# Sink-window attention and a gated feed-forward on one core: weight loads from GpSimd's queue, idle products at the start, and the first 256 tokens of all four sequences first

## Chip, cores and metric

One core of a Trainium2 chip. The metric is device time in microseconds of one execution of the program. Engines: PE (TensorE, products; PEld its weight loads), DVE (VectorE), ACT (ScalarE), POOL (GpSimd), SP (SyncE, which issues most transfers).

## The reference

Attention over 4 sequences x 8 heads x 768 tokens x 64 dimensions, float32. A token sees the first `n_sink` tokens and a window of the last `window` ones. Then a feed-forward over all 3072 tokens:

```
keep   = (col < n_sink) | ((0 <= row - col) & (row - col < window))
a      = softmax(where(keep, q @ k.T / 8, -1e9));  x = concat of heads of a @ v     # 3072 x 512
h      = x @ w_in                                # 512 x 2048
out    = (h * clip(h + 3, 0, 6) / 6) @ w_out     # 2048 x 512
```

`n_sink` (4) and `window` (128) are run-time values. The weights arrive as 64-bit floats.

## The kernel before

**Units and slots.** The tokens are cut into 12 units, a unit being 256 tokens of one sequence: (b, 0), (b, 1), (b, 2). A unit's 8 heads are taken as 4 pairs, and one pair of one unit is a *slot* of the attention, so there are 48 slots, `pus`. The list `units` sets their order: (0, 0) and (1, 0) lead, then sequence by sequence what is left. First units (u = 0) have 2 blocks of keys, scores of 128 and 256 columns for the two query tiles, and no sink part; later units have scores of 2 x 272 columns, a third block of keys, and the sinks by products of their own (`D_snk`, ssc, pz). Eight slots (s < 8, u = 0) are `plain`: they multiply in float32, which takes two passes a product. All others split each operand into two float32r parts, hi and lo (`split_parts`), by ACT and DVE, and copy K and Q within SBUF to both halves of the partitions (lines 247 and 260; K and Q have one buffer each).

**Order of the work.** A loop over s (line 534) runs the steps of one string; C is the scores and softmax of slot s - 1, E the products with V of slot s - 2, D the transposes of slot s - 1, L, V, Bk and Bq the loads and splits of slots s and s + 1, W the weight loads, and each "-" runs one step of the feed-forward:

```
ORDER = "V C00 - C01 E0 - C10 - C11 E1 L - Bk - Bq W - D0 - S D1 -"
MULT = [1] * 12
WN = [0, 1, 1, 1, 1, 4, 4, 4, 4, 4, 4, 4]
```

So there are 8 feed-forward steps a slot, taken from queues that a unit joins when its last pair has left E (line 528). A step is half of `ffn1` (12 products of 256 columns, hps, line 437) or half of `ffn2` (6 products of 512 columns, o, line 457); a unit has 34 steps. A step comes only when the weights that it needs have been placed in the program (line 496). What is left after slot 47 runs at the end, products alone.

**Weights.** 32 loads of 512 KB (`load_part`, lines 134 to 161): one in each of slots 1 to 4, four in each of slots 5 to 11. A load is issued by SP into one of three buffers st (shared with the output tile ost), and then turned from 64-bit into two float32r parts: two steps on ACT (lines 150 and 154), two on DVE (line 156, which moves the sign with a 16-bit AND, and line 158), the high part by ACT (line 35), the low part by DVE (line 161). SP's queue is in order; a load that waits for a free st stands ahead of the loads of kr, qr, vr (lines 217, 218, 232) and the copies of K and Q.

**Start.** GpSimd writes rel, col and the identity (lines 65 to 72); n_sink and window come by two transfers on ACT's queue (lines 79 and 80, tile raw); DVE makes the masks from them (lines 82 to 113), and GpSimd the masks m_t0 and m_t1 of the later units and two clearings (vs, ssc; lines 177 and 178). Seven small steps for the flag fl (lines 563 to 570), which chooses a general path at the end, run here too, as nothing holds them back.

Of the kernel before, what the change touches and what calls it, by code (L numbers as in the profile page):

```python
# [9 lines left out]
F32 = mybir.dt.float32  # L10
F32R = mybir.dt.float32r
I32 = mybir.dt.int32
BF16 = mybir.dt.bfloat16
U16 = mybir.dt.uint16
U32 = mybir.dt.uint32
ALU = mybir.AluOpType
AF = mybir.ActivationFunctionType
# [2 lines left out]
P = 128  # L20
SK = 16
WMAX = 128
SCALE = 0.125
BIG = 1.0e30


def split_parts(nc, hi, lo, src, hi_engine, lo_engine):

    copy_r(nc, hi_engine, hi, src)
    lo_engine.tensor_tensor(out=lo, in0=src, in1=hi.bitcast(F32), op=ALU.subtract)  # L30


def copy_r(nc, eng, out, src, scale=1.0):
    if eng is nc.scalar:
        nc.scalar.mul(out=out, in_=src, mul=scale)  # L35
    elif eng is nc.gpsimd:
        nc.gpsimd.tensor_scalar(out=out, in0=src, scalar1=scale, scalar2=1.0, op0=ALU.mult, op1=ALU.mult)
    elif scale != 1.0:
        nc.vector.tensor_scalar(out=out, in0=src, scalar1=scale, scalar2=None, op0=ALU.mult)
    else:  # L40
        nc.vector.tensor_copy(out=out, in_=src)  # L41
# [3 lines left out]
def attn_ffn_kernel(ctx: ExitStack, tc: tile.TileContext, qx, kx, vx, vfx, vsx, n_sink, window, w_in, w_out, out):  # L45
    nc = tc.nc
    B, NU, NP = qx.shape[0:3]
# [7 lines left out]
    const = ctx.enter_context(tc.tile_pool(name="const", bufs=1))  # L55
    fast = ExitStack()
    work = fast.enter_context(tc.tile_pool(name="work", bufs=2))
    ps = fast.enter_context(tc.tile_pool(name="ps", bufs=8, space=PSUM))
# [4 lines left out]
    relf = rel.rearrange("p a b -> p (a b)")  # L63
# [3 lines left out]
    nc.gpsimd.iota(colf[:, 0:P], pattern=[[1, P]], base=0, channel_multiplier=0,  # L67
                   allow_small_or_imprecise_dtypes=True)
    ident_r = const.tile([P, P], F32R, name="ident_r")
    ident0 = work.tile([P, P], F32, tag="st", name="ident0", bufs=3)  # L70
    make_identity(nc, ident0)
    nc.gpsimd.tensor_copy(out=ident_r, in_=ident0)
    ident = ident_r.bitcast(F32)
    three = const.tile([P, 1], F32, name="three")
    nc.vector.memset(three, 3.0)


    raw = const.tile([P, 2, 2], I32, name="raw")
    nc.scalar.dma_start(out=raw[:, 0, :], in_=n_sink.bitcast(I32).partition_broadcast(P))
    nc.scalar.dma_start(out=raw[:, 1, :], in_=window.bitcast(I32).partition_broadcast(P))  # L80
    rawf = const.tile([P, 2, 2], F32, name="rawf")
    nc.vector.tensor_copy(out=rawf, in_=raw)
    neg = const.tile([P, 2], F32, name="neg")
# [4 lines left out]
                                   op0=ALU.mult, op1=ALU.add)  # L88
# [3 lines left out]
    W2 = 2 * P + SK  # L92
    WP = 2 * P + 2 * SK
    m_t0 = work.tile([P, W2], BF16, name="m_t0", bufs=1)
    m_t1 = work.tile([P, W2], BF16, name="m_t1", bufs=1)
# [3 lines left out]
    own, prev, snk = relf[:, P:2 * P], relf[:, 2 * P:3 * P], colf[:, P:2 * P]  # L99
# [6 lines left out]
    def bias_from(dst, keep, engine=nc.vector):  # L106
        engine.tensor_scalar(out=dst, in0=keep, scalar1=-1.0, scalar2=BIG, op0=ALU.add, op1=ALU.mult)

# [2 lines left out]
    nc.vector.tensor_tensor(out=tmpm, in0=prev, in1=snk, op=ALU.max)  # L111
    bias_from(m_01[:, 0:P], tmpm)
    bias_from(m_01[:, P:2 * P], own)
    bias_from(m_t0[:, 0:P], prev, nc.gpsimd)
    bias_from(m_t0[:, P:2 * P], own, nc.gpsimd)
    bias_from(m_t0[:, 2 * P:W2], snk[:, 0:SK], nc.gpsimd)
    nc.gpsimd.tensor_copy(out=m_t1[:, 0:P], in_=m_t0[:, 0:P])
    nc.gpsimd.tensor_copy(out=m_t1[:, P:P + SK], in_=m_t0[:, 2 * P:W2])
    nc.gpsimd.tensor_copy(out=m_t1[:, P + SK:W2], in_=m_t0[:, P:2 * P])


    WIH = [const.tile([P, NP, 256], F32R, name=f"wih{i}") for i in range(NFP)]
# [6 lines left out]
    def weng(which, at):  # L129
        return {"D": nc.vector, "P": nc.gpsimd, "A": nc.scalar}[which[at % len(which)]]  # L130

    def load_part(hi, lo, src, rows, at):

        def like(t):
            return t.rearrange("p (a b) -> p a b", a=rows)

        if not wide:
            st = like(work.tile([P, 512], F32, tag="st", name="st", bufs=3))
            nc.sync.dma_start(out=st, in_=src)
            split_parts(nc, hi, lo, st, nc.scalar, nc.vector)  # L140
            return
        st = work.tile([P, 512, 2], I32, tag="st", name="st", bufs=3)
        nc.sync.dma_start(out=like(st.rearrange("p n w -> p (n w)")), in_=src.bitcast(I32))
        it = work.tile([P, 512], I32, tag="wt", name="wt", bufs=3)
        low, high = st[:, :, 0], st[:, :, 1]
        ft = it.bitcast(F32)
        half = st.rearrange("p n w -> p (n w)").bitcast(U16).rearrange("p (n w) -> p n w", w=4)


        nc.scalar.activation(out=ft, in_=high.bitcast(F32), func=AF.Abs, scale=2.0 ** -112)  # L150

        nc.scalar.activation(out=low, in_=low.bitcast(U32), func=AF.Copy, scale=2.0 ** -29 * (1 - 2.0 ** -18),
                             bias=7.5 * 2.0 ** -18 - 0.5)
        nc.vector.tensor_scalar(out=half[:, :, 1], in0=half[:, :, 3], scalar1=0x8000, scalar2=None,  # L156
                                op0=ALU.bitwise_and)
        nc.vector.scalar_tensor_tensor(out=it, in0=it, scalar=3, in1=low,  # L158
                                       op0=ALU.logical_shift_left, op1=ALU.bitwise_or)
        copy_r(nc, weng(WHI, at), hi, like(ft))  # L160
        weng(WLO, at).tensor_tensor(out=lo, in0=like(ft), in1=hi.bitcast(F32), op=ALU.subtract)  # L161
# [12 lines left out]

    vs = work.tile([P, NP, 4 * D], F32R, name="vs", bufs=1)
    ssc = work.tile([P, 2, P], F32R, name="ssc", bufs=1)
    nc.gpsimd.memset(vs.bitcast(F32), 0.0)
    nc.gpsimd.memset(ssc.bitcast(F32), 0.0)

    def batch_loads(b):  # L180
        v4 = vs[0:4 * SK].rearrange("p a (h d) -> p a h d", h=4)
# [10 lines left out]
    def eng(which, s):  # L192
        return {"D": nc.vector, "P": nc.gpsimd, "A": nc.scalar}[which[1 + (s % (len(which) - 1)) if s < START else 0]]

    first = [(0, 0), (1, 0)]
    units = first + [(b, u) for b in range(B) for u in range(NU) if (b, u) not in first]
    pus = [(b, u, p) for (b, u) in units for p in range(NP)]
    st_ = [dict() for _ in pus]
# [73 lines left out]
    def cell(s, h, t, c0, c1):  # L272

        if plain(s):
            return st_[s][f"P{h}"][:, t * P + c0:t * P + c1]
        return st_[s]["P"][:, h, t, c0:c1]
# [36 lines left out]
    def C_soft(s, h):  # L313
        b, u, p = pus[s]
        d = st_[s]
        nb, sm, rc = d["nb"], d["sm"], d["rc"]
        hs = slice(2 * h, 2 * h + 2)
        live = [(0, W2), (0, W2)] if u else [(0, P), (0, 2 * P)]
        for t in range(2):
            i, blk = 2 * h + t, cell(s, h, t, *live[t])  # L320
            nc.scalar.activation(out=blk, in_=blk, func=AF.Exp, scale=-1.0,  # L321
                                 bias=nb[:, i:i + 1], accum_out=sm[:, i:i + 1])
        nc.vector.tensor_scalar(out=sm[:, hs], in0=sm[:, hs], scalar1=1e-9, scalar2=None, op0=ALU.add)
        nc.vector.reciprocal(out=rc[:, hs], in_=sm[:, hs])  # L324
        for t in range(2):
            i, blk = 2 * h + t, cell(s, h, t, *live[t])
            norm((NORM0 if s < START else NORM)[i], blk, rc[:, i:i + 1])
        if u and h == 1:

            ss = ssc[:, :, 0:4 * SK].rearrange("p t (k h y) -> p t k h y", k=2, h=2)  # L330
            snk_in = d["P"].rearrange("p h t w -> p h (t w)")[:, :, 2 * P:2 * WP].rearrange(
                "p h (t y) -> p t h y", t=2)[:, :, :, 0:SK]
            split_parts(nc, ss[:, :, 0], ss[:, :, 1], snk_in, weng(SSE, 0), weng(SSE, 1))
# [181 lines left out]
    def slot_C(s, h, t):  # L515
        if 0 <= s < NS:
            C_score(s, h, t)
            if t == 1:
                C_soft(s, h)

    def slot_E(s, h):
        if 0 <= s < NS:
# [9 lines left out]
    WN = [0, 1, 1, 1, 1, 4, 4, 4, 4, 4, 4, 4]  # L532

    for s in range(NS + 2):
        for step in ORDER.split():
            if step == "-":
                drain(MULT[s] if s < len(MULT) else 1)
            elif step[0] == "C":
                slot_C(s - 1, int(step[1]), int(step[2]))
            elif step[0] == "E":  # L540
                slot_E(s - 2, int(step[1]))
            elif step == "V":
                if s < NS:
                    A_v(s)
                if 2 <= s and pus[s - 2][1:] == (1, 0):
                    batch_loads(pus[s - 2][0])
            elif step == "L" and s + 1 < NS and s > 0:
                A_kq(s + 1)
            elif step == "Bk" and 0 < s < NS:
                B_k(s)  # L550
            elif step == "Bq" and 0 < s < NS:
                B_q(s)
            elif step == "W":
                for _ in range(WN[s] if s < len(WN) else 0):
                    w_order.pop(0)()
            elif step[0] == "D" and 0 <= s - 1 < NS:
                D_pt(s - 1, int(step[1]))
            elif step == "S" and 0 <= s - 1 < NS:
                D_snk(s - 1)
    drain(sum(len(q) for q in queues))  # L560


    fl = const.tile([P, 4], F32, name="fl")
    nc.vector.tensor_scalar(out=fl[:, 0:1], in0=ns_f, scalar1=float(SK), scalar2=None, op0=ALU.is_gt)
    nc.vector.tensor_scalar(out=fl[:, 1:2], in0=win_f, scalar1=1.0, scalar2=None, op0=ALU.is_lt)
    nc.vector.tensor_scalar(out=fl[:, 2:3], in0=win_f, scalar1=float(WMAX), scalar2=None, op0=ALU.is_gt)
# [8 lines left out]
    with tc.If(flag == 1):  # L575
        with ExitStack() as gen:
# [71 lines left out]
            with tc.For_i(0, B, 1) as bi:  # L648
                for u in range(NU):
                    xn = gp.tile([P, NP, UT], F32, name="xn")  # L650
                    for c in range(NP):
                        nc.sync.dma_start(out=xn[:, c, :],
                                          in_=xv[ds(bi, 1), :, c, u * UT:(u + 1) * UT].rearrange("o p s -> (o p) s"))
# [75 lines left out]
```

## Time and profile before

| | us |
|---|---|
| median of 3 runs | 764.99 (764.61 to 767.12) |
| profiled execution | 765.18 |
| its span, first to last instruction | 763.3 |
| PE busy | 728.7 |
| DVE busy | 505.8 |
| ACT busy | 458.1 |
| POOL busy | 4.0 |

A busy PE need not be a PE at its peak: the ends of products are modelled and they overlap, so the number of products that start in a stretch tells more than the busy share. The granted clock is 1.00 at 2.4 GHz and 0.50 at 1.2 GHz. "Landing" is the end of a transfer after its issue.

### The profile page before, as it was taken

How to read it: one execution, taken by the hardware profiler on the slowest of the kernel's cores; microseconds unless marked ns; L12 is line 12 of the kernel's file. 1: busy time of each engine (PE TensorE's matmuls, PEld its weight loads, DVE VectorE, ACT ScalarE, POOL GpSimd, SP SyncE). 2: the span in 40 equal slices, each digit the busy share in tenths (PEclk: the TensorE clock that was granted, in tenths of full speed). 3: DMA queues.
4: the chain of work that ended last, by engine and by line, in shares of the span. 5: the costliest groups of instructions: out<-in, count | busy, mean ns of one | idle time of the engine just before them, and what ended most of it. 6: DMA issues, size and time to landing. Idle time of an engine off the chain costs nothing.

```text
span 763.3 us, 13907 instructions
## 1 busy us (share of the span) xinstructions
PE 728.7 (95%) x4832; PEld 648.1 (85%) x4832; DVE 505.8 (66%) x1434; ACT 458.1 (60%) x1115; POOL 4.0 (1%) x17
## 2 busy tenths in 40 slices
PE   4999888889999999999999999999999999999996
PEld 2677677679999999999889999899889989999895
DVE  4679999967677766765776776765676776542331
ACT  4788889776766755755666666755665665511211
POOL 2000000000000000000000000000000000000000
PEclk9999999999999999999999999999999999999998
DMA  5456878455454544532644545434554442000000
GB/s 187 121 165 217 238 212 237 138 142 132 128 134 122 134 125 105 140 95 67 166 110 114 143 107 127 120 82 102 146 130 116 128 114 72 15 15 1 28 1 32
DMA packets 57134, 89.87 MB, mean 118 GB/s; under 512 B 8672, under 2 KB 40416, under 8 KB 57056
## 3 DMA queue, kind: packets, MB, share of 16 engines
q1 hardware_dynamic: 56768, 88.90, 43.1%
q8 instruction: 40, 0.66, 0.4%
q14 instruction: 38, 0.31, 0.1%
q10 hardware_dynamic: 288, 0.00, 0.0%
HBM read 41.68 MB, written 6.29 MB: 63 GB/s over the span
## 4 chain that ended last, share of the span: by engine, by line
PE 78%; DVE 10%; ACT 5%; DMA 3%; issue 2%; SPq 1%; ACTq 0%; DVEq 0%
PE o L457 30%; PE hps L437 30%; PE av L399 7%; PE pt L341 4%; PE sp L297 4%; PE sp L292 2%; DMA K<-kt 1%; ACT Pt L307 1%; DVE st L156 1%; ACT Pt L321 1%; DVE wt L158 1%; DVE gf L444 1%; DVE Pt L299 1%; DMA raw<-in_window_dram 1%; DVE g L446 1%
## 5 line engine op out<-in xcount | busy, mean ns | idle before, releaser
L437 PE MATMUL hps<-xh,wih 128*128 128x256 f32 x768 | 219.9, 286 | 2.1 <-ACT wih L35 1.9
L437 PE MATMUL hps<-xh,wil 128*128 128x256 f32 x768 | 216.1, 282 | 1.6 <-DVE wil L161 1.6
L437 PE MATMUL hps<-xl,wih 128*128 128x256 f32 x768 | 215.5, 281 | 0.0
L457 PE MATMUL o<-woh,gh 128*128 128x512 f32 x384 | 156.2, 407 | 6.6 <-DVE gh L41 2.4
L457 PE MATMUL o<-woh,g 128*128 128x512 f32 x384 | 152.8, 399 | 1.9 <-DVE g L446 1.9
L457 PE MATMUL o<-wol,gh 128*128 128x512 f32 x384 | 152.5, 397 | 0.0
L437 PEld LDWEIGHTS hps<-xh,wih 128*128 128x128 f32 x768 | 145.7, 190 | 5.3 <-ACT wih L35 3.9
L437 PEld LDWEIGHTS hps<-xh,wil 128*128 128x128 f32 x768 | 145.2, 189 | 3.4 <-DVE wil L161 3.3
L437 PEld LDWEIGHTS hps<-xl,wih 128*128 128x128 f32 x768 | 145.6, 190 | 1.4
L321 ACT ACTIVATE Pt<-Pt,nb 128x272 f32<-128x272 f32 (+2 forms) x160 | 81.1, 507 | 73.3 <-DVE nb L299 71.3
L443 ACT ACTIVATE gf<-hps,three 128x512 f32<-128x512 f32 x96 | 65.9, 686 | 88.9 <-PE hps L437 88.4
L444 DVE SCALAR_TENSOR_TENSOR gf<-gf,hps 128x512 f32<-128x512 f32 x96 | 66.0, 687 | 67.0 <-ACT gf L443 65.8
L457 PEld LDWEIGHTS o<-woh,g 128*128 128x128 f32 x384 | 72.6, 189 | 21.8 <-DVE g L446 5.1
L457 PEld LDWEIGHTS o<-woh,gh 128*128 128x128 f32 x384 | 72.6, 189 | 19.1 <-DVE gh L41 3.1
L299 DVE CUSTOM_DVE_ANT_0 Pt<-sp,m_t 128x272 f32<-128x272 f32 x128 | 55.8, 439 | 49.5 <-PE sp L297 49.0
L307 ACT ACTIVATE Pt<-Pt,rc 128x272 f32<-128x272 f32 (+2 forms) x158 | 72.1, 502 | 25.9 <-DVE rc L324 24.7
L457 PEld LDWEIGHTS o<-wol,gh 128*128 128x128 f32 x384 | 72.6, 189 | 11.1 <-DVE wol L161 0.3
L446 DVE TENSOR_TENSOR g<-gf,gh 128x512 fp32r<-128x512 f32 x96 | 66.2, 690 | 1.1
L30 DVE TENSOR_TENSOR pl<-pt,ph 128x512 fp32r<-128x512 f32 (+1 forms) x80 | 52.8, 661 | 18.4 <-ACT ph L35 17.8
L297 PE MATMUL sp<-K,Q 128*128 128x272 f32 (+2 forms) x320 | 64.1, 288 | 0.7 <-DMA Q<-qt 0.4
L35 ACT ACTIVATE ph<-pt 128x512 fp32r<-128x512 f32 (+1 forms) x80 | 46.3, 578 | 29.5 <-PE pt L341 28.2
L297 PEld LDWEIGHTS sp<-K,Q 128*128 128x128 f32 x320 | 53.2, 189 | 8.1 <-DVE gf L444 0.7
(91 smaller groups left out, 944.0 us busy)
## 6 DMA issues: line engine op xcount, KB each, us to landing
K<-kt SPq DMA_DIRECT2D x128, 200.0 KB, 3.5
Q<-qt SPq DMA_DIRECT2D x160, 64.0 KB, 2.4
st<-in_w_in_dram SPq DMA_DIRECT2D x16, 512.0 KB, 4.7
st<-in_w_out_dram SPq DMA_DIRECT2D x16, 512.0 KB, 5.0
kr<-in_kx_dram SPq DMA_DIRECT2D x32, 200.0 KB, 2.6
qr<-in_qx_dram SPq DMA_DIRECT2D x48, 128.0 KB, 2.2
vr<-in_vx_dram SPq DMA_DIRECT2D x32, 192.0 KB, 2.6
out_dram<-ost SPq DMA_DIRECT2D x24, 256.0 KB, 2.3
```

The lines of the kernel that those rows point to most:

```text
L30: lo_engine.tensor_tensor(out=lo, in0=src, in1=hi.bitcast(F32), op=ALU.subtract)
L35: nc.scalar.mul(out=out, in_=src, mul=scale)
L297: nc.tensor.matmul(out=sp[:, 0:w], lhsT=Q[:, h, t * P:(t + 1) * P], rhs=K[:, h, part, k0c:k0c + w], start=(part == 0), stop=(part == 1))
L299: nc.vector.tensor_tensor_reduce(out=cell(s, h, t, 0, w), in0=sp[:, 0:w], in1=m[:, 0:w], scale=-SCALE, scalar=3.0e38, op0=ALU.add, op1=ALU ...
L307: nc.scalar.mul(out=blk, in_=blk, mul=c)
L321: nc.scalar.activation(out=blk, in_=blk, func=AF.Exp, scale=-1.0, bias=nb[:, i:i + 1], accum_out=sm[:, i:i + 1])
L399: nc.tensor.matmul(out=o, lhsT=l, rhs=r, start=(j == 0 and (h == 0 or not plain(s))), stop=(j == len(seq) - 1 and (h == 1 or not plain(s))))
L437: nc.tensor.matmul(out=hp[:, half, :], lhsT=l, rhs=r, start=(j == 0), stop=(j == n - 1))
L443: nc.scalar.activation(out=gf, in_=hp, func=AF.Relu, bias=three, scale=1.0)
L444: nc.vector.scalar_tensor_tensor(out=gf, in0=gf, scalar=6.0, in1=hp, op0=ALU.min, op1=ALU.mult)
L446: eng(GLO, state["n"] * NP).tensor_tensor(out=g, in0=gf, in1=gh.bitcast(F32), op=ALU.subtract)
L457: nc.tensor.matmul(out=acc, lhsT=l[:, f, ts_], rhs=r[i][:, f, :], start=(i == 0 and f == 0 and j == 0), stop=(i == NFP - 1 and f == 1 and ...
```

## The change

Weight loads are issued by GpSimd. Ten products of two 128x128 float32 tiles, whose result nobody reads, stand ahead of everything on PE, and ten more behind the scores and softmax of slot 0. The units (b, 0) of all four sequences lead, so slots 8 to 15 become first units that are not plain; which slots are plain is as before. `window` is loaded from SP's queue. The masks of later units and the two clearings are made at the top of s = 3. In the weights' conversion the sign is put in by one int32 step, (high AND -2^31) OR low, in place of the 16-bit one. Two tiles change their buffers: ident0 goes to kt's, fl to those of nb.

```
+WARM = (10, 10)
...
-    ident0 = work.tile([P, P], F32, tag="st", name="ident0", bufs=3)
+    ident0 = work.tile([P, P], F32, tag="kt", name="ident0", bufs=1)
...
+    def keep_busy(n):
+
+        idle = ps.tile([P, 512], F32, tag="bank", name="idle")
+        for _ in range(n):
+            nc.tensor.matmul(out=idle[:, 0:P], lhsT=relf[:, 0:P], rhs=relf[:, 0:P], start=True, stop=True)
+
+    keep_busy(WARM[0])
...
-    nc.scalar.dma_start(out=raw[:, 1, :], in_=window.bitcast(I32).partition_broadcast(P))
+    nc.sync.dma_start(out=raw[:, 1, :], in_=window.bitcast(I32).partition_broadcast(P))
...
-        nc.sync.dma_start(out=like(st.rearrange("p n w -> p (n w)")), in_=src.bitcast(I32))
+        nc.gpsimd.dma_start(out=like(st.rearrange("p n w -> p (n w)")), in_=src.bitcast(I32))
...
-        nc.vector.tensor_scalar(out=half[:, :, 1], in0=half[:, :, 3], scalar1=0x8000, scalar2=None,
-                                op0=ALU.bitwise_and)
+        nc.vector.scalar_tensor_tensor(out=low, in0=high, scalar=-2 ** 31, in1=low,
+                                       op0=ALU.bitwise_and, op1=ALU.bitwise_or)
...
+    def later_constants():
+
+        bias_from(m_t0[:, 0:P], prev, nc.gpsimd)
...
+        nc.gpsimd.tensor_copy(out=m_t1[:, P + SK:W2], in_=m_t0[:, P:2 * P])
+        nc.gpsimd.memset(vs.bitcast(F32), 0.0)
+        nc.gpsimd.memset(ssc.bitcast(F32), 0.0)
...
-    first = [(0, 0), (1, 0)]
+    first = [(b, 0) for b in range(B)]
...
             if t == 1:
                 C_soft(s, h)
+                if s == 0 and h == 1:
+                    keep_busy(WARM[1])
...
     for s in range(NS + 2):
+        if s == 3:
+            later_constants()
...
-    fl = const.tile([P, 4], F32, name="fl")
+    fl = work.tile([P, 4], F32, tag="nb", name="fl", bufs=3)
```

## Rows read from the trace of the kernel before

**Rows 1.** The page, part 1: busy time, share of the span and instructions of each engine.

```profile
PE 728.7 (95%) x4832; PEld 648.1 (85%) x4832; DVE 505.8 (66%) x1434; ACT 458.1 (60%) x1115; POOL 4.0 (1%) x17
```

**Rows 2.** The table of stretches: us from A to B, length, then PE, PEld, DVE, ACT and POOL busy (in brackets: instructions), the granted clock of TensorE, the DMA share and GB/s.

```profile
0.00:50.00 50.00, 37.71 (x115) 25.40 (x116) 28.34 (x113) 31.80 (x83) 3.98 (x17) 1.00 0.51 157
50.00:80.00 30.00, 29.74 (x175) 23.76 (x174) 27.70 (x73) 26.21 (x61) 0.00 (x0) 1.00 0.64 199
80.00:165.00 85.00, 72.29 (x446) 60.16 (x445) 76.07 (x190) 69.08 (x159) 0.00 (x0) 0.96 0.70 202
165.00:655.00 490.00, 487.23 (x3451) 447.54 (x3450) 335.88 (x992) 311.37 (x781) 0.00 (x0) 1.00 0.46 117
...
98.50:154.50 56.00, 50.05 (x323) 41.74 (x323) 51.78 (x126) 46.36 (x103) 0.00 (x0) 1.00 0.68 198
```

**Rows 3.** The chain of waits from 128 to 165 us: start, length, what.

```profile
132.95 6.03 DMA K<-kt
...
139.03 3.96 DMA vr<-in_vx_dram
```

**Rows 4.** SP's own waits from 80 to 140 us: who waited for whom: us in total, times, longest us.

```profile
SPq L143 <- DVE wt L158: 12.8, 6, 5.2
```

**Rows 5.** Instructions in order of time, at the start: start us, us, engine, line, operation, out<-in, count, and in brackets the idle time before and what ended it.

```profile
0.75 0.40 SPq L217 DMA_DIRECT2D kr<-in_kx_dram  x1
...
0.84 0.24 POOL L65 IOTA rel<- 128x128 f32 x1 [0.39 <-POOLq L712]
...
5.72 1.66 PE L292 MATMUL sp<-kr,qr 64*128 64x128 f32 x8 [5.72 <-DMA qr<-in_qx_dram]
6.05 0.17 DVE L82 CAST rawf<-raw 128x4 f32<-128x4 int32 x1 [5.18 <-DMA raw<-in_window_dram]
...
6.86 0.15 DVE L564 TENSOR_SCALAR fl<-nw 128x1 f32<-128x1 f32 x1
...
7.56 0.28 DVE L101 TENSOR_SCALAR rel<-rel,nw 128x128 f32<-128x128 f32 x1
...
9.50 0.28 DVE L299 CUSTOM_DVE_ANT_0 Ph<-sp,m 128x128 f32<-128x128 f32 x1
...
11.98 1.36 PE L341 MATMUL pt<-ident_r,Ph 128*128 128x128 f32 x4 [4.60 <-DVE Ph L309]
```

**Rows 6.** Four products of attention times V of plain slots, at two times: columns as in rows 5.

```profile
33.27 1.65 PE L399 MATMUL av<-pf,VF 128*128 128x256 f32 x4
...
76.40 0.92 PE L399 MATMUL av<-pf,VF 128*128 128x256 f32 x4
```

**Rows 7.** A stretch of 10 us and one of 2.5 (columns as in rows 2), and single PE products (columns as in rows 5).

```profile
30.00:40.00 10.00, 8.99 (x26) 5.67 (x25) 5.03 (x20) 7.85 (x20) 0.00 (x0) 1.00 0.41 129
...
84.00:86.50 2.50, 2.50 (x7) 1.97 (x6) 2.25 (x8) 2.50 (x6) 0.00 (x0) 0.50 0.66 226
...
49.05 0.41 PE L437 MATMUL hps<-xh,wih 128*128 128x256 f32 x1
...
49.57 0.28 PE L437 MATMUL hps<-xh,wih 128*128 128x256 f32 x1
49.69 0.28 PE L437 MATMUL hps<-xl,wih 128*128 128x256 f32 x1
...
83.28 0.53 PE L457 MATMUL o<-woh,gh 128*128 128x512 f32 x1 [2.14 <-DVE sm L323]
```

**Rows 8.** DMA issues by line (count, KB each, median us to landing), and the weight loads from 60 to 150 us: duration of the issue in ns min/median/max, first and last start, and the landing of these loads.

```profile
raw<-in_n_sink_dram ACTq DMA_DIRECT2D x1, 1.0 KB, 3.1
raw<-in_window_dram ACTq DMA_DIRECT2D x1, 1.0 KB, 4.8
...
L143 SPq DMA_DIRECT2D st<-in_w_out_dram x11: 327/328/805, 60.0 to 138.5; - x11
...
DMA to landing us min/median/max: 3.6/5.2/6.8
```

**Rows 9.** DVE's groups of instructions over the whole span, each shape apart: line, engine, operation, names, shapes, count, then busy us, mean ns of one, and idle us before.

```profile
L299 DVE CUSTOM_DVE_ANT_0 Pt<-sp,m_t 128x272 f32<-128x272 f32 x128 | 55.8, 439 | 49.5 <-PE sp L297 49.0
L30 DVE TENSOR_TENSOR pl<-pt,ph 128x512 fp32r<-128x512 f32 x64 | 44.0, 688 | 16.5 <-ACT ph L35 16.1
...
L156 DVE TENSOR_SCALAR st<-st 128x512 uint16<-128x512 uint16 x32 | 24.0, 750 | 3.4 <-ACT st L154 3.1
L158 DVE SCALAR_TENSOR_TENSOR wt<-wt,st 128x512 int32<-128x512 int32 x32 | 22.0, 689 | 0.5
L30 DVE TENSOR_TENSOR kt<-kr,kt 128x400 fp32r<-128x400 f32 x32 | 18.2, 568 | 4.3 <-ACT kt L35 4.2
...
L30 DVE TENSOR_TENSOR pl<-pt,ph 128x384 fp32r<-128x384 f32 x16 | 8.9, 553 | 1.8 <-ACT ph L35 1.7
L30 DVE TENSOR_TENSOR ssc<-Pt,ssc 128x64 fp32r<-128x64 f32 x32 | 7.2, 224 | 1.0
L299 DVE CUSTOM_DVE_ANT_0 Pt<-sp,m 128x256 f32<-128x256 f32 x16 | 6.8, 422 | 12.4 <-PE sp L297 12.4
...
L41 DVE CAST ssc<-Pt 128x64 fp32r<-128x64 f32 x32 | 6.1, 190 | 7.8 <-ACT Pt L307 7.7
...
L299 DVE CUSTOM_DVE_ANT_0 Pt<-sp,m 128x128 f32<-128x128 f32 x16 | 4.6, 286 | 1.8 <-PE sp L297 1.8
...
L30 DVE TENSOR_TENSOR kt<-kr,kt 128x256 fp32r<-128x256 f32 x8 | 3.4, 420 | 1.2 <-ACT kt L35 1.2
```

More of the change, by code (lines that the diff above doesn't have):

```diff
@@ L13 @@
 BF16 = mybir.dt.bfloat16
-U16 = mybir.dt.uint16
 U32 = mybir.dt.uint32
@@ L113, in attn_ffn_kernel @@
     bias_from(m_01[:, P:2 * P], own)
[L114 to L119, printed above, removed]
     WIH = [const.tile([P, NP, 256], F32R, name=f"wih{i}") for i in range(NFP)]
@@ L146, in load_part @@
         ft = it.bitcast(F32)
-        half = st.rearrange("p n w -> p (n w)").bitcast(U16).rearrange("p (n w) -> p n w", w=4)
         nc.scalar.activation(out=ft, in_=high.bitcast(F32), func=AF.Abs, scale=2.0 ** -112)
@@ L176, in attn_ffn_kernel @@
     ssc = work.tile([P, 2, P], F32R, name="ssc", bufs=1)
-    nc.gpsimd.memset(vs.bitcast(F32), 0.0)
-    nc.gpsimd.memset(ssc.bitcast(F32), 0.0)
+    def later_constants():
+        bias_from(m_t0[:, 0:P], prev, nc.gpsimd)
+        bias_from(m_t0[:, P:2 * P], own, nc.gpsimd)
+        bias_from(m_t0[:, 2 * P:W2], snk[:, 0:SK], nc.gpsimd)
+        nc.gpsimd.tensor_copy(out=m_t1[:, 0:P], in_=m_t0[:, 0:P])
+        nc.gpsimd.tensor_copy(out=m_t1[:, P:P + SK], in_=m_t0[:, 2 * P:W2])
+        nc.gpsimd.tensor_copy(out=m_t1[:, P + SK:W2], in_=m_t0[:, P:2 * P])
+        nc.gpsimd.memset(vs.bitcast(F32), 0.0)
+        nc.gpsimd.memset(ssc.bitcast(F32), 0.0)
     def batch_loads(b):
```

## The prediction, made before the change was run

> **What bounds the kernel now.** I read the page first: TensorE is busy for 728.7 us of the span of 763.3 us [rows 1], so only what keeps it waiting, or makes it slow, is worth anything. The table of stretches then tells where that is [rows 2]. From 165 to 655 us 3451 products start in 490 us, 7.04 per us, and PE is busy for 487.2: this part is bound by products, and nothing of the change reduces them. From 80 to 165 us only 446 start in 85 us, 5.2 per us, while DVE is busy for 76.1 of 85. At the later pace 446 products take 63 us, so some 20 us are lost here (a rough figure, as the mix of shapes differs a little). Within it, from 98.5 to 154.5, DVE is busy for 51.8 of 56 us: the weights are still being converted (four loads in each of slots 5 to 11) beside the attention of slots 8 to 11, which are not "plain". From 50 to 80 us, DVE is as busy, but so is PE.
>
> The chain of waits shows what fills the rest of that stretch: K lands after 6.03 us and then vr after 3.96 us, both on SP's queue [rows 3]. SP's own waits from 80 to 140 us hold 12.8 us in which it stood at a weight load for a free st buffer [rows 4], with K, Q, vr, kr and qr queued behind.
>
> The first 50 us are lost otherwise. The scores of slot 0 are there at 7.4 us, but the mask is not; the first softmax step comes at 9.50 and the first transpose at 11.98 [rows 5]. From there on PE is nearly always busy, but slowly: four av products take 1.65 us at 33 us and 0.92 us at 76 us [rows 6]. The column of the granted clock says 1.00 there; the durations say the lower level (1.2 GHz), and I go by them. It ends at 49.3 us, under the first hps products, whose 256 columns go from 0.41 to 0.28 us. Later, after 2.14 us of idleness, the column itself shows 0.50 (84 to 86.5) [rows 7].
>
> **The change part by part.** The sum is made against the profiled execution, 765.18 us (span 763.3), 0.19 above the median of 764.99.
>
> *The start.* n_sink took 3.1 us to land and window, behind it on ACT's queue, 4.8 [rows 8]. On SP's queue window goes out first, at 0.75, where kr does now; at 3.1 to 4.8 us it lands at 3.9 to 5.6 instead of 6.0 [rows 5]. It pushes kr and qr back by one issue (0.4 us). The seven fl steps, which stood in the mask chain from 6.86 to 7.56, get a tile of the nb rotation, and so go to the end, under the products of the last units; 0.7 us go. The mask could thus be ready 1.1 to 2.8 us earlier. The masks m_t0 and m_t1 and the two clearings are first needed by slot 16 now, and lie on a GpSimd that does nothing else but loads: nothing, and if that cover failed, a weight load behind them would be late by less than GpSimd's whole 4.0 us [rows 1]. ident0 takes the buffer of kt, which slot 8 is the first to use: nothing. But the second ten idle products stand between slot 0's last score and its first transpose. Each is two passes of 128 float32 columns; four av products are 768 columns in such passes, so one idle product is 0.55 us at the low level, up to 5.5 us for ten, less the overlap of their ends [rows 6]. From 7.8 us they end at some 12 to 13, against 11.98 now. The first ten need rel alone, which is there at 1.1 us [rows 5]; they run to about 6.5, while the scores get their data at 6.1 at the earliest. So the gain in the mask is spent: 0, with bounds of -2.5 and +1.5.
>
> *Does it lift the clock?* No row shows float32 products raising it: from 30 to 40 us PE was busy for 8.99 of 10 us with such products and transposes and stayed slow, and it rose only under hps [rows 7]. I take it that it stays low. The Trainium skill ("TensorE: Matmul & The Clock Gate", Part 1) says the opposite for matmul activity in general: that it releases the throttle and that idle gaps bring it back. By it the idle products would do their work; this is the first rival.
>
> *Slots 1 to 4.* With st always loaded ahead, ACT and DVE wait less: PE's idle share of 10% [rows 7] over the 34 us from 12 to 46 bounds this at -3.4; I take -0.5, since these gaps end with softmax results, which stay as they are.
>
> *The bit step.* The 16-bit step (750 ns) becomes an int32 step like the next one (689 ns) [rows 9]. It reads two strided operands where that one reads one, so 689 to 750; I take 689. On 16 loads in the DVE-bound stretch: -1.0; elsewhere DVE has room.
>
> *The order.* Slots 8 to 15 are now first units. For each DVE saves, by [rows 9]: L299 4 x 439 against 2 x 286 + 2 x 422, 0.34 us; pl 2 x (688 - 553), 0.27; kt 568 - 420, 0.15; ssc 190 + 224, 0.41: 1.17 us a slot, 4.7 us on slots 8 to 11. But PE's work moves too: 6016 columns in a later unit's slot, counted from the code (scores 8 x 272, av 2 x 1280, 8 transposes of 128, sinks 256), against 3840 (scores 4 x 384, av 2 x 768, 6 transposes), at 0.12 us for 256 columns [rows 7] 1.0 us a slot, 4.1 us that is done later at PE's pace. Left: -0.6. Bounds: -4.7 (if PE had no room for it anyhow) and +1. K and vr are smaller too, which belongs to the next term.
>
> *The queue.* Weight loads (all 32) leave SP for GpSimd's queue, where nothing stands behind them but other loads and, once, the late constants. SP's 12.8 us of waits go [rows 4]. What is late next is the buffer of K, since there is only one. At most the 10 us of the chain come back [rows 3], at least nothing, as DVE is 92% busy meanwhile. I take -4.0, near DVE's own idle time in that stretch (4.2 us of 56), because DVE's work is the row that sets the floor. That loads are issued by GpSimd no row prices; the nearest is the landing of SP's weight loads, 3.6 to 6.8 us [rows 8]. With three buffers a microsecond more is hidden: 0, and the case beyond it is a rival.
>
> Sum: 0 - 0.5 - 1.0 - 0.6 - 4.0 = -6.1, so 759.
>
> **The rivals.** *The clock does rise* (0.22). The idle products bring the array to 2.4 GHz before slot 1. For it: the trace has no stretch of float32 products on all 128 rows alone; those before were mixed with 64-row scores and transposes. Against: some 35 us of them without a rise. Then ACT, busy for 7.85 of 10 us [rows 7], is next, and the 34 us shrink by at most 21%, 7.3 us; I take -7 beside the rest of the sum: 752. If the clock falls back between slots, the gain is some 2 us, and within the forecast's range.
>
> *The transfers were hidden anyway* (0.17). DVE's 92% are the bound, and SP's waits only fell beside it; K's own buffer makes the wait again. Without the queue's term and that of slots 1 to 4: -1.6, so 763.5, within what a measurement can tell.
>
> *Weights come late from GpSimd* (0.13; slower). Place: 60 to 140 us. 11 loads of w_out were issued from 60.0 to 138.5 [rows 8], with one of w_in between two of them in the mean, so one load in 3.9 us; with three buffers a load may take 11.8 us from its issue to the end of its conversion. The landing takes 5.2 now, which leaves 6.6 for ACT and DVE. It decides once landing plus conversion exceed 11.8, so with conversions of about 5 us (two steps each on ACT and DVE, DVE's of 0.69 and 0.75 us [rows 9], and a turn to wait for on both; an estimate) from a landing of 7 us. At a landing of 10 us each load comes 1.1 us later, some 21 us over 20 loads, less the 6 gained; of these 15 I let half be caught, as a second unit's products can run meanwhile: about 773. The Trainium skill ("SBUF — State Buffer", SBUF: two separate sides) gives a reason: descriptors for such loads are written by GpSimd, which DVE's faster copies lock out of a shared port. No row here shows it, as GpSimd issues nothing yet.
>
> **How the numbers follow.** The forecast has 0.45, the clock 0.22, hidden transfers 0.17, late weights 0.13; 0.03 are left for what I don't see. A measurement of this kernel tells about 0.3%, 2.3 us: faster is below 762.7, slower above 767.3. Faster: nine tenths of the forecast's 0.45, the clock's 0.22 and a fourth of the hidden case, 0.67. Same: 0.18. Slower: 0.15. Range: the forecast's own is 753 to 764; with the clock's 752 and its bound, and the lower part of late weights, 749 to 769.
>
> **What would show it.** Right: no wait of SP at a weight load; DVE's busy time from 98.5 on smaller by a microsecond a slot, with products at over 5.8 per us (now 323 in 56 us); av at 1.65 us still at 30 us; first transpose at about 12 us. Wrong: av at 0.92 us in slots 1 to 4 (the clock rival); ACT's first weight step waiting for st (late weights); K's and vr's landings on the chain as before (hidden). A loss after 165 us would contradict everything here: nothing was moved into that part but 1 us a slot of PE's own work.

## The result: slower, 770.8 us against 765.9

The changed kernel takes 770.78 us (median of 5 runs, 769.72 to 773.76), the kernel before 765.87 beside it (5 runs); the ratio is 1.0072, 95% interval 1.0052 to 1.0091. The forecast was 759. The profiled execution of after, the slowest of its five, took 773.76 us (span 771.9), that of before 765.18 (span 763.3).

The table of stretches of the changed kernel, columns as in [rows 2]:

```profile
0.00:50.00 50.00, 41.17 (x170) 30.28 (x171) 28.91 (x107) 31.17 (x84) 8.65 (x26) 0.73 0.49 155
50.00:80.00 30.00, 26.01 (x133) 19.39 (x131) 26.02 (x67) 24.07 (x58) 4.49 (x9) 0.96 0.61 191
80.00:165.00 85.00, 71.46 (x420) 62.03 (x419) 68.87 (x181) 62.90 (x151) 8.16 (x15) 0.91 0.60 170
165.00:655.00 490.00, 488.38 (x3447) 450.44 (x3446) 340.74 (x992) 314.12 (x779) 0.00 (x0) 1.00 0.47 123
```

The loss is made from 50 to 165 us. From 50 to 80, 133 products start where 175 did [rows 2]; from 80 to 165, 420 for 446, though these slots now hold less PE work (of the 170 in the first 50 us, 40 are passes of the idle products). DVE went from 76.1 to 68.9 us of 85 and ACT from 69.1 to 62.9: no engine is as full any more as DVE was, all of them wait. After 165 us PE is as full as before (488.4 of 490), so nothing is lost there but work moved into it.

Who waits for whom: us in total, times, longest us. First ACT from 0 to 170 us, before and after; then PE from 40 to 170 us, before and after.

```profile
ACT wt L150 <- DMA st<-in_w_out_dram: 1.8, 2, 1.1
```

```profile
ACT wt L151 <- DMA st<-in_w_in_dram: 11.4, 5, 5.9
ACT wt L151 <- DMA st<-in_w_out_dram: 8.0, 7, 1.7
```

```profile
PE hps L437 <- ACT wih L35: 1.9, 3, 0.9
```

```profile
PE hps L447 <- ACT wih L35: 10.1, 6, 2.7
```

ACT stands 19.4 us at the first conversion step of a weight whose load has not landed (before 2.4, with 0.6 of w_in). The first 5.9 of them, up to 8.4 us, cost little, as the first softmax step is not ready before 10.8; 13.5 lie from 40 us on. PE stands 10.1 us before an hps product because wih is not converted. How that looks on DVE, ACT and PE, in order of time (columns as in [rows 5]):

```profile
73.36 0.16 DVE L334 RECIPROCAL rc<-sm 128x2 f32<-128x2 f32 x1
...
75.50 0.66 ACT L151 ACTIVATE wt<-st 128x512 f32<-128x512 f32 x1 [1.70 <-DMA st<-in_w_out_dram]
76.07 0.49 ACT L317 ACTIVATE Ph<-Ph,rc 128x256 f32<-128x256 f32 x1
76.47 0.61 ACT L35 ACTIVATE wih<-wt 128x512 fp32r<-128x512 f32 x1
...
77.13 0.39 PE L447 MATMUL hps<-xh,wih 128*128 128x256 f32 x1 [2.37 <-ACT wih L35]
```

The factor rc that the softmax step L317 needs is there at 73.52, yet ACT starts that step only at 76.07: a conversion stands ahead of it, idles 1.70 us for its load and then runs. Behind the softmax step stands the high part of a wih, and PE idles 2.37 us for it. ACT started nothing else while it stood: it took its steps in the order of its list, which is made when the program is built. The loads themselves are not later: over loads 8 to 31 a landing takes 4.9 us in the mean (before 5.0), and one load ends its conversion every 3.90 us (before 3.86); but from the start of a load's first ACT step to the start of its combining step on DVE there are 4.6 us in place of 3.4 (worked out from the records of each load).

The start, and the clock:

```profile
1.13 4.64 PE L81 MATMUL idle<-rel 128*128 128x128 f32 x20 [1.13 <-POOL rel L65]
...
6.37 0.17 DVE L90 CAST rawf<-raw 128x4 f32<-128x4 int32 x1 [5.49 <-DMA raw<-in_n_sink_dram]
...
7.21 0.93 PE L302 MATMUL sp<-kr,qr 64*128 64x128 f32 x8 [1.45 <-DMA qr<-in_qx_dram]
...
8.07 2.50 PE L81 MATMUL idle<-rel 128*128 128x128 f32 x20
...
8.10 0.21 DVE L115 TENSOR_SCALAR m<-rel 128x128 bf16<-128x128 f32 x1
...
8.65 0.23 DVE L115 TENSOR_SCALAR m<-col 128x128 bf16<-128x128 f32 x1
...
9.30 1.48 DVE L115 TENSOR_SCALAR m<-col 128x128 bf16<-128x128 f32 x1
9.50 0.95 POOL L187 MEMSET vs<- 128x1024 f32 x1
...
10.38 0.31 POOL L188 MEMSET ssc<- 128x256 f32 x1
...
12.85 0.45 PE L351 MATMUL pt<-ident_r,Ph 128*128 128x128 f32 x1 [2.28 <-DVE Ph L319]
```

The idle products did bring the array to the higher level: slot 0's scores take 0.93 us, not 1.66 [rows 5]. But it does not last:

```profile
19.20 1.65 PE L409 MATMUL av<-pf,VF 128*128 128x256 f32 x4
23.36 0.82 PE L409 MATMUL av<-pf,VF 128*128 128x256 f32 x4
24.96 0.92 PE L409 MATMUL av<-pf,VF 128*128 128x256 f32 x4
30.07 1.65 PE L409 MATMUL av<-pf,VF 128*128 128x256 f32 x4
```

Stretches of the changed kernel cut at the changes of the granted clock (columns as in [rows 2]):

```profile
5.80:12.60 6.80, 3.36 (x28) 2.87 (x28) 5.60 (x24) 2.39 (x8) 3.17 (x9) 1.00 0.91 332
12.60:22.90 10.30, 10.03 (x30) 6.68 (x30) 5.88 (x24) 7.62 (x22) 0.53 (x1) 0.50 0.46 142
22.90:29.70 6.80, 5.12 (x25) 3.32 (x24) 5.61 (x20) 6.14 (x18) 0.53 (x1) 1.00 0.48 138
29.70:46.80 17.10, 14.82 (x43) 9.87 (x42) 9.10 (x36) 10.94 (x32) 1.59 (x3) 0.50 0.36 117
77.50:84.30 6.80, 6.80 (x28) 5.64 (x27) 5.34 (x13) 4.67 (x13) 0.69 (x2) 0.50 0.68 207
```

The array falls back to the lower level at 12.6 us, after 3.36 us of work in 6.8, rises at 22.9 and falls again at 29.7. The rise at 22.9 comes without idle products, after 10.03 us of attention's own float32 products and transposes in 10.3. It is also at the lower level from 77.5 to 84.3, right behind the wait of 2.37 us of hps for wih. From 50 to 170 us the clock's records hold 20.5 us at the lower level, before 6.9: the new waits on PE seem to cost a second time.

### The profile page after: what moved, and what is told of

Read it like the earlier page. It is cut to its first block, busy times and chain, and to the rows that moved or that the text cites. A ratio compares the mean times of both kernels' runs of the same rounds, so it can differ in the third digit from the quotient of the medians.

```text
span 771.9 us, 13996 instructions
## 1 busy us (share of the span) xinstructions
PE 737.0 (95%) x4872; PEld 661.5 (86%) x4872; DVE 507.5 (66%) x1434; ACT 456.3 (59%) x1115; POOL 21.3 (3%) x49
## 4 chain that ended last, share of the span: by engine, by line
PE 79%; DVE 6%; ACT 6%; DMA 5%; issue 2%; SPq 1%; DVEq 0%; ACTq 0%; POOLq 0%
PE hps L447 31%; PE o L467 30%; PE av L409 7%; PE pt L351 5%; PE sp L307 5%; PE sp L302 2%; DMA st<-in_w_in_dram 1%; ACT Pt L331 1%; ACT Pt L317 1%; DMA st<-in_w_out_dram 1%; DMA raw<-in_n_sink_dram 1%; DMA Q<-qt 1%; PE spt L370 1%; DVE gf L454 1%; ACT gf L453 1%
## 5 line engine op out<-in xcount | busy, mean ns | idle before, releaser
L447 PE MATMUL hps<-xh,wih 128*128 128x256 f32 x768 | 223.4, 291 | 11.1 <-ACT wih L35 10.1
L447 PE MATMUL hps<-xh,wil 128*128 128x256 f32 x768 | 220.1, 287 | 0.3 <-DVE wil L162 0.3
L447 PE MATMUL hps<-xl,wih 128*128 128x256 f32 x768 | 219.0, 285 | 0.0
L447 PEld LDWEIGHTS hps<-xh,wih 128*128 128x128 f32 x768 | 147.8, 192 | 16.9 <-ACT wih L35 13.5
L447 PEld LDWEIGHTS hps<-xh,wil 128*128 128x128 f32 x768 | 147.8, 192 | 1.4 <-DVE nb L309 0.7
L447 PEld LDWEIGHTS hps<-xl,wih 128*128 128x128 f32 x768 | 147.5, 192 | 1.2
L317 ACT ACTIVATE Pt<-Pt,rc 128x272 f32<-128x272 f32 (+2 forms) x158 | 72.1, 503 | 26.7 <-DVE rc L334 25.4
L467 PEld LDWEIGHTS o<-wol,gh 128*128 128x128 f32 x384 | 72.7, 189 | 10.8
```

What stands on the lines that cost most here:

```text
L317: nc.scalar.mul(out=blk, in_=blk, mul=c)
L447: nc.tensor.matmul(out=hp[:, half, :], lhsT=l, rhs=r, start=(j == 0), stop=(j == n - 1))
L467: nc.tensor.matmul(out=acc, lhsT=l[:, f, ts_], rhs=r[i][:, f, :], start=(i == 0 and f == 0 and j == 0), stop=(i == NFP - 1 and f == 1 and ...
```

## Experiments

Medians of 5 to 12 runs; the kernel before, run beside them, took 765.35 to 765.49. "Conversion" is ACT's and DVE's work on one weight load.

| run | us | ratio to before, 95% | ACT's wait for weight landings, 0 to 170 us | PE's wait for converted weights, 40 to 170 us |
|---|---|---|---|---|
| before | 765.4 | | 2.4 | 4.8 |
| after | 770.78 | 1.0052-1.0091 | 19.4 | 10.4 |
| e1 queue alone | 779.54 | 1.0165-1.0212 | 24.3 | 16.0 |
| e2 after, SP's queue | 765.54 | 0.9989-1.0010 | 16.6 | 4.3 |
| e3 order alone | 756.05 | 0.9848-0.9887 | 3.6 | 5.5 |
| e4 after, no idle products | 772.12 | 1.0073-1.0101 | 12.1 | 12.7 |
| e5 = e4 on SP's queue | 759.66 | 0.9908-0.9936 | 12.1 | 7.8 |
| e6 idle products alone | 770.70 | 1.0059-1.0102 | 12.6 | 10.9 |
| e7 order, bit step | 760.77 | 0.9930-0.9960 | 7.4 | 8.6 |
| e8 ACT's queue alone | 803.20 | 1.0473-1.0512 | 11.3 | 23.7 |
| e9 = e1, late conversions | 772.05 | 1.0071-1.0110 | 19.0 | 9.9 |
| e10 = e3, late conversions | 754.75 | 0.9849-0.9887 | 1.7 | 6.9 |
| e11 = e7, late conversions | 758.51 | 0.9896-0.9947 | 6.8 | 3.3 |
| e12 = e5, 16-bit step | 759.16 | 0.9893-0.9931 | 10.4 | 6.2 |
| e13 = e10, K and Q on GpSimd's queue | 767.26 | 1.0000-1.0041 | 3.9 | 9.1 |
| e14 = e10, 10 + 10 idle products | 765.82 | 0.9986-1.0016 | 12.8 | 11.2 |
| e15 = e10, 4 + 4 idle products | 766.19 | 0.9997-1.0023 | 4.2 | 12.1 |

The two columns of waits are sums of rows of one trace each (ACT's: before the first conversion step; PE's: for wih, woh, wil, wol, wt and st); those of e11 and e13 are of executions of 764.5 and 772.0 us, above their medians. The last column goes with the time, though the gap is narrow: 3.3 to 8.6 us in kernels of up to 765.6, 9.1 to 16.0 in those of 765.8 to 780, 23.7 in the slowest. Within the first two groups it ranks nothing.

From 40 us on alone, ACT's waits for landings are 12.1 to 22.1 us in the four kernels with the weights on GpSimd's queue (after, e1, e4, e9), 11.3 in e8 and 1.2 to 8.6 in all others. The rest of that column lies in the first 40 us.

**One part alone, or all but one (e1 to e4).**

```
e1: -nc.sync.dma_start(out=like(st.rearrange(     on before
    +nc.gpsimd.dma_start(out=like(st.rearrange(
e2: the reverse, on after
e3: -first = [(0, 0), (1, 0)]                     on before
    +first = [(b, 0) for b in range(B)]
e4: no keep_busy                                  on after
```

> The kernel before with one edit: all weight loads leave on GpSimd's queue. Theory (the queue: GpSimd's queue issues a load only when its buffer is free, and the list of ACT's steps now has conversions that stand at its head before the load has landed, so that ACT, and PE behind it, waits for landings): ACT waits for weight landings some 10 to 20 us in all in place of 2.4, and the time is 769 to 772 beside 766 for the kernel before. Rival 1 (the order of the units costs the time): 764 to 767, as this kernel keeps the old order. Rival 2 (the idle products cost it, by a late start and by a clock that falls back): 762 to 767. The forecast's own term for the queue (-4): 762.

> The changed kernel with the weight loads back on SP's queue, all else kept. Theory (the queue): most of the loss goes, 760 to 764, and ACT's waits for weight landings fall from 19.4 us to under 6. Rival 1 (order of the units): 769 to 772 as the changed kernel. Rival 2 (idle products): 769 to 772.

> The kernel before with one edit: the first 256 tokens of all four sequences come first. Theory (the queue): the order is worth little, 764 to 767 (the forecast's -0.6, with -4.7 and +1 as its ends). Rival 1 (the order costs the time, as slots 8 to 15 have less PE work in them to cover the weights' conversion, and 1 us a slot of PE's work is done later): 769 to 772. Rival 2 (idle products): 764 to 767.

> The changed kernel without the 20 idle products, all else kept. Theory (the queue): the idle products are worth some 1 to 3 us through the clock (scores of slot 0 at 0.93 us in place of 1.66, some av products at 0.9), less 1 us of a later start; without them 770 to 773. Rival 1 (order): the same, 770 to 773. Rival 2 (the idle products cost the time, by the late start, by a list of ACT's steps that has three conversions ahead of the first softmax, and by a clock that falls back): 761 to 766.

The queue alone costs 14.1 us, more than my theory had; the order alone gains 9.4, which no theory had; taking the queue out of the changed kernel gives back only 5.2, and ACT's waits stay at 16.6 us (8.6 of them from 40 us on) where I had under 6. The idle products are worth 1.3 us in the changed kernel, less than its runs scatter; 772.12 for e4 is what the theory and rival 1 both had. That an edit of the queue alone changes the lists is seen in e1: leaving out the table load and the reading of sums, its order of ACT's 922 steps differs from before's from the 90th on. The order and the queue together leave -9.4 + 14.1; e2 at 765.54, with the order and SP's queue, says that something else in the change eats the order's 9.4. One place is the start, on ACT:

```profile
9.80 0.66 ACT L151 ACTIVATE wt<-st 128x512 f32<-128x512 f32 x1 [7.34 <-DMA st<-in_w_in_dram]
...
11.66 0.67 ACT L151 ACTIVATE wt<-st 128x512 f32<-128x512 f32 x1 [0.66 <-DMA st<-in_w_in_dram]
...
12.93 0.70 ACT L151 ACTIVATE wt<-st 128x512 f32<-128x512 f32 x1
...
14.59 0.40 ACT L331 ACTIVATE Ph<-Ph,nb 128x128 f32<-128x128 f32 x1
```

Three conversions stand ahead of the first exp, which so starts at 14.6 us; in after it starts at 10.84. Most of this is made up again: at equal feed-forward work (within one product) e2 is behind e5, the same kernel without idle products, by 7.6 us when slot 6's first reciprocal starts (77.2 against 69.6), by 2.6 at slot 7's (89.0, 86.4), and by 5.6 at slot 16's (213.7, 208.1). So what stays lost is lost after 89 us.

**What eats the order's gain (e5 to e7), and a queue that is not GpSimd's (e8).**

```
e5: e2 and e4 in one
e6: + keep_busy(10) at both places                on before
e7: e3, and
    -tensor_scalar(half[:, :, 1], half[:, :, 3], 0x8000, bitwise_and)
    +scalar_tensor_tensor(low, high, -2 ** 31, low, bitwise_and, bitwise_or)
e8: nc.scalar.dma_start for the weights           on before
```

> The changed kernel with the weight loads on SP's queue and without the 20 idle products: the order of the units, the bit step, the late constants, window on SP's queue and the late fl are left of the change. Theory A (the idle products cost some 6 to 9 us, as they put three conversions of weights ahead of the first softmax step in ACT's list: that step ended at 16.3 us in the kernel with them and at 11.2 without): 755 to 759. Theory B (the bit step, the late constants or the moved loads eat what the order brings): 763 to 767.

> The kernel before with the 20 idle products alone. Theory A (they cost time through the lists): the first softmax step later by 1 to 5 us, 768 to 774. Rival (they bring the array to the higher clock in slots 1 to 4 and shorten them): 758 to 763. The forecast (they do nothing but take up the time that the mask gains, and here the mask gains nothing): 766 to 770.

> The kernel before with two edits: the order of the units, and the int32 bit step. The order alone gave 756.05. The forecast's term for the bit step is -1.0 with ends of -2 and 0: 754 to 756. If the step is nearer its other end (750 ns), or DVE is no longer the bound where the weights are converted: 756 to 757. If the int32 step is dearer (it waits for ACT's second step, which the 16-bit step does as well): 757 to 760.

> The kernel before with the weight loads on ACT's queue, which is served as SP's is, but is a queue of its own. Rival M (any second queue makes loads and the small moves of K and Q share the DMA engines, so that K and Q land late: K took 7.0 us in the median on 50 to 160 us with GpSimd's queue, 3.7 before): K again at 6 to 7 us, time 772 to 782. Rival G (loads that GpSimd issues come late or land late): K stays at 3.5 to 4.5 us, and the time is 764 to 772, the rest being ACT's own waits at the issue for a free buffer.

The idle products cost 5.3 us alone, as theory A had it, and 5.9 in e2 against e5 (765.54 - 759.66; e5 itself just above theory A's 759). e7 was a surprise: the int32 step is the cheaper one in its row, 689 ns for 750 as forecast, and the kernel with it is 4.7 us slower than e3. DVE's group in after, answering to L156 in [rows 9]:

```profile
L157 DVE SCALAR_TENSOR_TENSOR st<-st 128x512 int32<-128x512 int32 x32 | 21.9, 689 | 6.6 <-ACT st L155 6.6
```

What differs is the order on ACT. From 21.5 us on, e3 has (left) and e7 has (right):

```
hi wih<-wt                      Abs wt<-st   (next load)
norm Ph                         hi wih<-wt
Abs wt<-st                      norm Ph
low st<-st                      low st<-st
pf<-pt                          Abs wt<-st   (the load after)
exp Ph                          pf<-pt
```

One DVE step put in place of another, 61 ns shorter, moves two conversions ahead of attention's steps on another engine, and PE's wait for wih goes from 4.9 to 8.6 us (before as after, from 40 to 170 us; e3, then e7):

```profile
PE hps L437 <- ACT wih L35: 4.9, 3, 2.9
```

```profile
PE hps L437 <- ACT wih L35: 8.6, 7, 1.9
```

e8 tells of the queues: count, KB each, median us to landing, 50 to 160 us, in before, e1 and e8.

```profile
K<-kt SPq DMA_DIRECT2D x20, 200.0 KB, 3.7
Q<-qt SPq DMA_DIRECT2D x20, 64.0 KB, 2.9
```

```profile
K<-kt SPq DMA_DIRECT2D x16, 200.0 KB, 7.0
Q<-qt SPq DMA_DIRECT2D x16, 64.0 KB, 5.0
```

```profile
K<-kt SPq DMA_DIRECT2D x12, 200.0 KB, 6.5
Q<-qt SPq DMA_DIRECT2D x12, 64.0 KB, 5.8
```

With before's order of units and the loads on another queue, K and Q, still on SP's, land later by 2.1 to 3.3 us: rival M as far as landings go. e8's time is no measure of that, as ACT also comes late to the issues (over loads 8 to 31 one goes out 5.7 us in the mean after its buffer is free, in before 1.3). With the new order it is otherwise: by the same view K's median is 3.8 us in after and 3.8 in e2, 2.5 in e4 and 2.8 in e5; only Q is later, 4.0 against 2.1 in both pairs.

**The same instructions, other lists (e9 to e12).**

```
e9, e10, e11:   load_part only issues the load; its conversion
                steps are written LAG loads later (2 in e9, 1 else)
-                if q[0][0] <= 4 * NFP - len(w_order):
+                if q[0][0] <= done[0]:
+    if len(waiting) > LAG:
+        convert_one()
e12: e5 with the 16-bit step of before
```

> The first experiment's kernel (weights on GpSimd's queue, 779.5) with the four conversion steps of each load written two loads later in the program, so that they stand later in the lists. Theory L (the time is lost because conversions stand at the head of ACT's list before their load has landed): ACT's waits for landings fall from 24 us to under 8, and the time to 764 to 772. Rival M (a second queue makes loads and the moves of K and Q collide on the DMA engines): K still lands in 5.5 us or more and the time stays at 775 to 782. Both at once: 770 to 776, with both signs.

> The kernel with the order of the units alone (756.05), with the conversion of each load written one load later: the same instructions, only the lists differ. Theory L: ACT's waits for landings (3.6 us) go below that, and the time moves by up to 5 us either way with the waits of hps for wih, 752 to 760. If lists are worth nothing: 755 to 757.

> Order and int32 bit step (760.77), with the conversion of each load written one load later. Theory L (the int32 step is no dearer, it only gave a list in which ACT waits 7.4 us for landings in place of 3.6): 753 to 757 with ACT's waits under 4 us. Rival (the int32 step itself costs the 4.7 us): 759 to 762.

> The changed kernel with the weight loads on SP's queue, no idle products and the 16-bit step: the order, the late constants, window on SP's queue and the late fl remain. With the int32 step it took 759.66. If the 16-bit step is better by itself: 755 to 757. Theory L (the step only shuffles the lists): anything from 754 to 763, in step with ACT's waits for landings (12.1 us with the int32 step, 7.0 of it in one wait).

A feed-forward step, which came once its weights' load was placed, now comes once their conversion is (`done`), so PE's list changes as well as ACT's and DVE's.

e9 gives back 7.5 of the queue's 14.1 us with the same loads on the same queue. PE's wait for weights falls from 16.0 to 9.9, ACT's for landings only from 24.3 to 19.0, where I expected under 8; K still lands after 7.4 us (by the same view). So new lists are worth 7.5 us on this queue; whether the other 6.6 lie in lists as well, or in the later landings, is not separated. e10 is no faster than e3 by its interval. e11 gains 2.3 us on e7 and falls between theory and rival; beside e10, its like with the 16-bit step, the int32 step still costs 3.8 us. In e5 against e12 it costs 0.5. So its cost is 4.7, 3.8 or 0.5 us, by the kernel around it: 4.7 is not a price of its own, but that its own price is nothing is not shown. e12 does not test theory L, whose 754 to 763 left room for nearly any time.

**What was still open (e13 to e15).**

```
e13: nc.gpsimd.dma_start for K and Q              on e10
e14: keep_busy(10), keep_busy(10)                 on e10
e15: keep_busy(4), keep_busy(4)                   on e10
```

> The fastest kernel so far (order, conversions one load later, 754.75) with the moves that build K and Q on GpSimd's queue and the weights still on SP's. Rival M (two queues make loads and moves collide on the DMA engines): K lands in 5 us or more in place of 3.4, Q in 4 or more in place of 2.1, and the time is 760 to 770. If the queue's cost lies in the weight loads alone (late issue, conversions at ACT's head): K lands in under 4.5 us, 753 to 758.

> The same fastest kernel with 10 and 10 idle products. In its list of ACT's steps one conversion of a weight stands ahead of the first softmax step, and that load lands at some 13 us. Theory (the idle products cost by this list): the first softmax ends at 14 to 15 us in place of 11.2, the time is 757 to 762, though scores and av products of slots 0 and 1 run at the higher clock. If the higher clock pays for it: 751 to 755.

> The same with 4 and 4 idle products, with which the list has no conversion ahead of the first softmax step. Theory: the first softmax ends at 11 to 12 us as without them, and the time is 752 to 757 (what the clock brings in the first slots is lost again if it falls back at 14 us). Rival (idle products cost by standing on PE ahead of the scores and the first transposes): 756 to 760.

e13 falls between: the time is rival M's (767.3), Q lands after 5.2 us as M has it (in e10 2.1), but K after 3.3 (in e10 3.4). And it need not be a collision with loads: from 220 to 640 us, with no weight load left, Q still takes 4.4 us in the median on GpSimd's queue, and 2.6 in e10 on SP's. So e13 does not show what M says. In e14 the first softmax ends as late as I had it (its first reciprocal starts at 14.2 us, in e10 at 11.2), but the time is above all that I had. e15 refutes my theory of the idle products: no conversion stands ahead of the first softmax, whose reciprocal starts at 11.2 us as in e10, and the kernel is still 11.4 us slower. PE's waits from 40 to 170 us, e10 and then e15:

```profile
PE hps L448 <- ACT wih L36: 3.3, 5, 1.7
PE o L468 <- ACT woh L36: 2.7, 1, 2.7
```

```profile
PE hps L457 <- ACT wih L37: 6.6, 5, 1.9
PE o L477 <- ACT woh L37: 4.5, 3, 2.6
```

On the chip itself the products did next to nothing there (e15's start):

```profile
1.13 2.08 PE L83 MATMUL idle<-rel 128*128 128x128 f32 x8 [1.13 <-POOL rel L67]
5.59 1.66 PE L312 MATMUL sp<-kr,qr 64*128 64x128 f32 x8 [2.38 <-DMA qr<-in_qx_dram]
7.18 2.07 PE L83 MATMUL idle<-rel 128*128 128x128 f32 x8
11.83 1.36 PE L361 MATMUL pt<-ident_r,Ph 128*128 128x128 f32 x4 [2.57 <-DVE Ph L329]
```

They are over at 9.25 us, the scores take 1.66 us as without them, so the clock has not risen, and the first transpose is on time. The loss is made from 50 us on, in PE's waits for conversions, with ACT's waits for landings at 4.2 us only. What differs by then is the lists: ACT's order departs from e10's at its 9th step. That this is what costs the time is argued, not shown, and why three kernels with the products (e6, e14, e15) all get bad lists stays open.

## Why the prediction was wrong

Along kernels that differ by one part each the 5.4 us (against 765.4; 4.9 against the 765.87 beside it) come as follows: order -9.4 (e3), bit step +4.7 (e7), late constants, window, fl and ident0 -1.1 (e5), queue +12.5 (e4), idle products -1.3 (after; within the scatter). The parts don't add in another order (the idle products are worth -1.3, +5.3, +5.9 or +11), so a price holds only beside the lists in which it was measured.

- **The queue, -4.0: the step that failed.** SP's 12.8 us at weight loads did go:

```profile
SPq L227 <- DVE kt L30: 13.0, 3, 6.9
SPq L270 <- PE sp L307: 10.8, 1, 10.8
SPq L270 <- ACT wt L151: 9.4, 1, 9.4
```

  These are SP's waits in after from 80 to 140 us, answering to [rows 4]: none is at a weight load, and SP waits elsewhere. They bought nothing: K (4.38 us) and vr (2.77) are still on the chain [rows 3]. From 45 to 170 us three weight loads stand on it, where before had one, of 3.64 us at 101.1:

```profile
52.78 5.70 DMA st<-in_w_in_dram
69.09 6.39 DMA st<-in_w_out_dram
129.02 5.58 DMA st<-in_w_in_dram
```

  The term took the time of K and vr on the chain as won and put the issuing by GpSimd at nothing. I had asked what is late next on SP, and not what the new queue does to the order in which ACT meets the loads. Measured: +14.1 alone, +12.5 and +5.2 beside the rest. How much of it is ACT's order and how much late landings of K and Q is open; in the changed kernel K does not land later, Q does by 1.9 us.
- **The rival of late weights** had the place (60 to 140 us) and nearly the time (773), but not the mechanism: it needed landings over 7 us, and they take 4.9. Conversions stand at ACT's head before their load lands all the same. The descriptors that the Trainium skill ("SBUF — State Buffer", SBUF: two separate sides) has DVE hold up would show as longer landings; in after they are not longer (4.9 against 5.0), in e1 a little (5.5). e1's longest, 10.4 us, is no sign of it, as e8 has the same on ACT's queue.
- **The order, -0.6: right in sign, far too small.** In e3 slot 12's first reciprocal starts at 156.8 us (before 164.5), slot 16's at 207.6 (before 220.7), and from there to slot 47's it takes 435.0 us (before 429.6). So 13.1 us are won and 5.4 paid back. I had 4.7 and 4.1, for slots 8 to 11 only: the DVE rows gave the steps, but not that waits behind them may shrink too; slots 12 to 15 are 5.4 us shorter as well, as much as is paid back later. The new order brings new lists too, and no run parts the two, so the 9.4 may hold a share of lists.
- **The clock: the forecast was wrong that it stays low, the rival that it stays high.** Ten idle products on all 128 rows do lift it (1.00 from 5.8 us in after; in e6 only from 7.3, behind scores of 1.66 us), as the Trainium skill ("TensorE: Matmul & The Clock Gate", Part 1) says of matmul activity in general. It falls back at 12.6 us, behind the idle time before the first transposes. I had priced that case at 2 us; e4 gives 1.3, which the scatter covers. The column's 1.00 ahead of 49.4 us in before, which I set aside for the durations, is no measurement: the trace's first clock record lies at 49.4.
- **The start, 0 with -2.5 to +1.5:** it lost 0.9 (first transpose at 12.85 for 11.98 [rows 5]). n_sink, not window, is now the last to land, at 6.34, while two weight loads are in flight from 1.4 us on (they land after 6.9 and 8.0 us). The late constants, which I had at nothing, do not run in slot 3 but at 7.8 us, on a GpSimd that has nothing ahead of them, and DVE's L115 beside them takes 1.48 us where its neighbours take 0.21 and 0.23. It ends at 10.78, 0.09 after GpSimd's last clearing. In e4 the same step takes 1.38 us beside the same clearings; in e2, where the long clearing is over at 2.3 us, 0.26. The Trainium skill ("SBUF — State Buffer", SBUF: two separate sides) has a GpSimd instruction and a DVE instruction in a mode with two ports lock each other out of a shared pair of ports. These rows agree, though no row shows DVE's mode.
- **The bit step, -1.0:** the duration was right (689), the effect was not: +4.7, +3.8 or +0.5, by the kernel around it.
- **Signs named beforehand:** av at 0.92 us early (seen, at 25 us), ACT waiting for st (seen, 19.4 us), K and vr on the chain (seen): three of the "wrong" signs. Of the "right" ones SP's waits at loads are gone and av takes 1.65 us at 30.07, but from 98.5 to 154.5 only 298 products start, 5.3 per us, where I wanted over 5.8. The loss after 165 us that would have contradicted everything did not come.

The term of slots 1 to 4 (-0.5) can't be told from the clock's part: slot 4's first reciprocal starts at 44.5 us for 45.5.

## What to carry to other kernels

Where a builder, and not the kernel, sets the order of each engine's list, an edit is not priced by the rows it changes alone: take the new list of the engine next to the bound and look which step now stands at its head before its data can be there. Test a doubtful edit together with a shuffle that changes no instruction (here, conversions written a load or two later; 7.5 us on e1, 2.3 on e7, nothing clear on e3): if that moves the time as much as the edit does, the edit's own effect is not known. Of this change only the order of the units is worth keeping: e3 (756.05) or e10 (754.75) is faster than both kernels, by 9 to 11 us than before and 15 to 16 than after.

## Not expected of the hardware

- Loads moved from SP's queue to another one, GpSimd's or ACT's, landed about as fast as before (4.2 to 5.6 us in the median for 512 KB against 4.7 to 5.3; single ones up to 10.4 against 6.8), while the small moves left on SP's queue slowed down: K from 3.7 to 7.0 and 6.5, Q from 2.9 to 5.0 and 5.8. With the order changed too (after, e4) only Q did.
- One DVE step took 1.48 us (1.38 in e4), its like 0.21 and 0.23, beside a clearing of 128x1024 on GpSimd.
- After a wait of PE of 2.37 us the granted clock was 0.50 for 6.8 us (77.5 to 84.3) although PE was busy for all of them.
